# Packed attention and a three-way maximum layer on one core: the first two batches written in another order with other engines, and the steady batches written as one list for all engines

## The chip, the cores and the metric

The kernel runs on one core of a Trainium2 chip. The metric is the device time of one execution in microseconds (us). Before the change three runs took 495.62, 495.81 and 496.78 us.

In this text PE is the matrix engine (TensorE), DVE the vector engine, ACT the scalar engine, POOL GpSimd, and SP the engine that issues the DMAs. PSUM is the memory that PE writes its results to, SBUF the other on-chip memory.

## The reference

`q`, `k` and `v` have 8 batches, 8 heads, 576 positions and 64 columns; `p` has 32 packed queries per head. The packed queries attend to the 576 keys; every position's query then attends to the 32 packed results, which serve as keys and as values. The result, 4608 rows of 512, goes through a layer that takes the largest of three products and multiplies it by an output matrix:

```python
p_packed = sm_attn(p, k, v)
out = sm_attn(q, p_packed, p_packed)
x = out.transpose(0, 2, 1, 3).reshape(B * S, H * D)
h = np.maximum(np.maximum(x @ w1, x @ w2), x @ w3)   # 512 -> 768
return h @ w_out                                     # 768 -> 512
```

`sm_attn` is softmax attention with scale 1/8. All data is float32.

## The kernel before

**The work of one batch.** It is cut into stages, each a Python generator that issues a step at every `next`. A letter names the stage in the written order; the first digit behind it is the batch.

- S (`scores`): the packed queries against the keys, 32 narrow matmuls into two PSUM tiles, one for each parity r of the heads.
- A (`weigh`, and for batches 0 and 1 `turn`): maximum on DVE, exponential with its sum on ACT; in batches 0 and 1 a transposition on PE and copies out of PSUM. Z (`invert`): 1/sum on DVE.
- X (`spread`, batches 2 and on): two transpositions on DVE and 16 small DMAs that bring the weights into the layout of the value product.
- V (`values`): 80 narrow matmuls with v, scaled on DVE. K (`packed`): one transposition on PE and a copy. Q (`queries`): the packed results against q, 32 narrow matmuls.
- B (`attend`), for each r, eleven steps: transpositions (DVE), maximum (DVE), subtraction, exponential (ACT), sum (DVE), adding 1e-9, reciprocal (DVE), multiplication by it, transposition (DVE), rounding to a high part, and the low part as a difference. High and low part together carry float32 through fast matmuls.
- P (`project`), for each of six blocks j of the 768 hidden columns: the packed results times the three weights of that block, 16 narrow matmuls, then a high part on ACT and a low part on DVE. So the weights meet 32 packed rows instead of 576.
- N (`layer_in`), for each j six steps of six wide matmuls (two halves of the positions, three weights). E (`maximum`): a copy out of PSUM and two maxima on DVE, for each half.
- H (`halves`): sums and differences of pairs of blocks and their high and low parts, named ya, yb and yc. O (`layer_out`): 14 steps of nine wide matmuls on these (seven products in place of eight for each block of 2 by 2, in two columns m). F (`finish`): scaling and sums of the 14 results, and four stores.

Beside the batches, C (`convert`) makes float32 out of the weights' 64-bit words in four steps (ACT, ACT, DVE, POOL), and W (`weights`) prepares the output matrix's seven operands. k, v, q and w in the order are loads, issued by SP. I sets how many dummy matmuls on the identity PE does ahead of the next group.

**What sets the order.** The first two batches, with the start of the third and all weights, are a written list of words, `START`; the list is run under a manual schedule, so every engine's instructions stand in its order. A letter v, g or a behind a word puts that step on DVE, POOL or ACT in place of its default. Batches 2 to 7 go through a loop with a clock: each tick is one step of N or O, and `STAGES` says at which tick a stage of the next batch comes due (S at 7, X at 12, V at 29, Q at 36). There only PE's order is manual; the scheduler orders the other engines by its own estimate, and every step runs on its default engine: copies and casts on ACT (`copy`, L120 and L122), low parts on POOL (`split_lo`, L125), the subtraction of the maximum on POOL (L387), the multiplication by 1/z on DVE (L401), the differences in H on POOL (L505).

**Buffers.** PSUM has two pools: `ps_big`, two buffers of two banks, and `ps_moe`, four buffers of one bank, in which the results of N and O turn. A result's buffer comes free with the last instruction on DVE or ACT that reads it. Loads, hidden blocks and the spread weights share eight SBUF buffers (tag b), so a load can have to wait until an earlier product is through.

Of the kernel before, what the change touches and what calls it, by code (L numbers as in the profile page):

```python
# [22 lines left out]
P = 128  # L23
G = 2
# [24 lines left out]
k00 k01 I10 S0 A01 w02 w00 v00 C02 C02 A01 q010 A00 v01 A00 I7 A01 q000 A00 A01v A00v C02 q001 V01 C00 C00 V00  # L49
Z01 V01 Z00 V00 K0 K0v I1 Q0 w01 B000 C02 B010 C00 C01 C01 C01 q011 B010 B010 B010 B000 B000v B000 k10 C01 I8  # L50
Q0 B011 k11 B001 B001 B000 B000v w12 B010 C12 B000 B000 w11 I4 S1 v10 C00 I3 P00 B000 B000g v11 B001 w10 A10
A10 B001 B011 B011 B011 B010v q10 q11 A11 B010 P00 B001 B001 P00 P00 w21 A11 P00 k20 B010g B010 C12 C12 B000
I10 N00 C12 k21 A10 w20 Z10 B011 A10 w22 B010v B010 B011v B011 A11 A11 V101 B011g B001 C10 B001 w30 N00 C11
Z11 V101 C10 C10 C10 B011 C11 C11 C11 B001 B001v K1 B001 K1 Q1 B10 B011 B11 E000v C21 w32 B011v N00 E000 P01
P01 B11 C21 N00 N00 N00 P01 C21 S2 C21 E000 E001v E001 C20 C20 C20 C20 A20 C22 C22 N01 w42 N01 C22 E010 A20
w31 A21 E001 A21 C30 E010 C22 N01 N01 E010 w40 B10 C30 w41 P02 P02 C30 E011v P10 N01 P02 E011 C32 C32 N01 N02
C30 N02 C32 C32 C31 C31 C31 E011 X2 P10 C40 C40 N02 N02 w51 C31 B11v P10 E020v B10 C41 C41 C41 w50 P03 w62 C42
C42 C42 E020 v21 P03 C40 P11 P03 C50 E021 N02 N02 C41 v20 w52 E021 N03 E020 C40 N03 C51 E021 C42 B10 P04 E030v
C51 C51 w64 B10 w63 B11 B11 B11v X2 H00 C51 E030 N03 B10 B10 B11 P04 P04 H00g N03 E031 E030 N03 N03 E031 H01g
B11g X2 E031 N04 C64 B10 B10 B10g B10 H00 C52 N04 N04 B11 E040 N04 E040 E040 C50 B11v B11v C50 N04 P11 P11 C50  # L60
C63 C52 E041 C64 N04 N10 N10 E100 E100 w60 E041 C62 C63 C62 E041 H04 C52 H02 N10 N10 C52 w65 Z20 Z21 E101 N10
H02 C63 N10 N11 V201 C60 q20 P05 P05 C63 C62 E101 N11 V201 K2 K2 E101 C64 C64 E110v E110 P05 E100 q21 C62 H04v
W1v W1 H02v W1 N11 N11 E111 C65 C65 C65 N11 N11 E110 w61 Q2 B21 H03g C65 W1 W1 N05 N05 C60 B20 E050 N05 E050
H03v W2v W2v C61 C61 P12 C61 P12 P13 E111 C60 P13 N05 E051 N05 N05 P12 E051 E051 N12 C61 B20 C60 E111 N12 E050
P14 E120v N12 E120 P13 E120 W1 W1 H01v W0 W2 W2 H04 W0 B20v H01 P14 W0v W0g W0 H03v P14 N12 N12 N12 W1 N13 W2v
W2 W0v P20 H01 P15 E130 E121v E121 E121 N13 N13 E130 W0 N13 E131 E130 W1g W2v W2v H03 P15 P15 N13 k30 N13 E131
E131 N14 B20 N14 N14 E140 O0 H03g N14 H05v F0 E140 B20 B20v N14 N14 E141 N15 E141 E141 E140 O0 F0 O0 B21 B21
O0 B21 H13g H05 H05 H03v H05 N15 H01v E150 H01v B21 E150 N15 N15 E150 E151 W1v W0 H14 B20 H05g W2 H10v H10v
B21v B21 F0 N15 E151 P20 N15 E151 H14g H15 O0 O0 H05v O0 H13v W0g H11 F0 F0 O0 F0 W0v H12 O0 W2 F0 H11 F0 B21
O0 O0 F0 F0 O0 F0 F0 F0 F0 O0 O0 H12 H14 H10v H11v H11 H12v B20 H13 O1 H15v H15v H15v H13 H13v F1 O1 O1 H13  # L70
H15v F0 H11 F0 H11v H15v F1 F1 O1 O1 F1 B21 O1 F1 F1 O1 F1 O1 O1 F1 F1 k31 B21 B21v P20 B20 B20v O1 O1 B20v O1
O1 F1 F1 F1 F1 F1 O1 F1 F1
# [3 lines left out]
STAGES = "S1:7 P3:7 v1:9 X1:12 P4:18 P5:18 q1:26 V1:29 k2:31 K1:33 Q1:36 P6:40 P7:40 P8:45"  # L76
# [3 lines left out]
def fused_kernel(ctx: ExitStack, tc: tile.TileContext, kp, qt, va, vb, wi, wo, out):  # L80
# [529 lines left out]
    with tc.manual_schedule():  # L610
        for word in START.split():
# [5 lines left out]
            elif kind in loads:  # L617
                loads[kind](*x)
            else:
                if name not in begun:  # L620
                    begun[name] = stages[kind](*x)
                next(begun[name], None)
    chosen[0] = None


    clock, due = [0], []

    def begin(stage, at):
        due.append([at, len(due), stage])

    def tick():

        while True:
            ready = [d for d in due if d[2] is not None and d[0] <= clock[0]]
            if not ready:
                break
            d = min(ready, key=lambda d: d[:2])
            wait = next(d[2], None)
            while wait == 0:
                wait = next(d[2], None)  # L640
            if wait is None:
                d[2] = None
            else:
                d[0] = clock[0] + wait
        clock[0] += 1

    def both(f, b):
        def steps():
            for g in range(G):
                f(b, g)  # L650
            yield 0
# [92 lines left out]
```

## Time and profile before

| | before |
|---|---|
| median of three runs | 495.81 us (495.62 to 496.78) |
| the profiled execution | 495.07 us |
| its span, first to last instruction | 493.3 us |
| mean granted PE clock | 0.988 |
| PE busy | 469.0 us, 95% of the span |
| PE weight loads busy | 407.4 us, 83% |
| DVE busy | 319.3 us, 65% |
| ACT busy | 192.2 us, 39% |
| POOL busy | 286.1 us, 58% |

The span is 1.77 us shorter than the time of the execution that it was taken from. A view by line or tile gives for each group of instructions its tiles (out<-in, without buffer numbers), its shape, its count, its busy time, the mean of one, and after the bar the idle time of the engine ahead of it with what ended most of that. The view of waits says which engine and line waited for which, the total, the count and the longest. The chain of work starts at the last instruction and goes back at each step to what released it, or to the instruction ahead of it on its engine. The table of stretches gives each engine's busy time in a part of the span, with the number of instructions.

### The profile page before, as it was taken

Reading aid. Unit: us, or ns where it says so; the run is one execution under the profiler, and the core shown is the slowest. Engines: PE = TensorE matmul, PEld = TensorE weight load, DVE = VectorE, ACT = ScalarE, POOL = GpSimd, SP = SyncE. Lnnn points to the kernel's source line nnn. Section 1 sums busy time; section 2 is a strip of 40 time slices with the busy share of each in tenths; the row PEclk is TensorE's granted clock in tenths of the full one; section 3 lists DMA queues with packets and bytes.
Section 4 is the critical chain, followed back from the end, with each engine's and each line's share of the span. In section 5 each row is a group of like instructions: output and inputs, shape, how many; then the busy total and the mean of one; then the engine's idle time right before and its main releaser. Section 6 shows DMA issues by size and latency. Waiting matters only on the chain.

```text
span 493.3 us, 11594 instructions
## 1 busy us (share of the span) xinstructions
PE 469.0 (95%) x4710; PEld 407.4 (83%) x4710; DVE 319.3 (65%) x625; ACT 192.2 (39%) x374; POOL 286.1 (58%) x229
## 2 busy tenths in 40 slices
PE   8879988979887999999999999999999999999997
PEld 3347786768877989899998989899998999899996
DVE  2798997897987664586457565576457564673522
ACT  4266854322310153424434253524434353423430
POOL 0464868694971257652755566652756566644672
PEclk9998999899998999999999999999999999999999
DMA  8996846010013426015440426015430423011002
GB/s 314 385 398 246 269 133 228 3 52 2 25 48 94 163 44 190 35 37 157 99 155 25 145 55 209 17 49 151 114 133 25 152 53 110 3 58 41 1 0 97
DMA packets 36581, 55.67 MB, mean 113 GB/s; under 512 B 17328, under 2 KB 27568, under 8 KB 36528
## 3 DMA queue, kind: packets, MB, share of 16 engines
q1 hardware_dynamic: 36528, 54.93, 34.1%
q8 instruction: 37, 0.61, 0.5%
q14 instruction: 16, 0.13, 0.1%
HBM read 41.94 MB, written 9.44 MB: 104 GB/s over the span
## 4 chain that ended last, share of the span: by engine, by line
PE 76%; DVE 12%; DMA 5%; POOL 2%; ACT 2%; issue 2%; SPq 1%; DVEq 0%; ACTq 0%; POOLq 0%
PE mi L467 41%; PE mo L536 23%; PE pw L431 6%; DMA v<-in_va 2%; PE av L329 2%; PE s L358 2%; DMA q<-in_qt 1%; PE s L243 1%; DMA wi<-in_wo 1%; DVE r L481 1%; DVE r L505 1%; DVE ybl L125 1%; DVE ycl L125 1%; DVE pl L444 1%; ACT wi L178 1%
## 5 line engine op out<-in xcount | busy, mean ns | idle before, releaser
L467 PE MATMUL mi<-a2h,ph 128*128 128x288 f32 x576 | 175.8, 305 | 4.8 <-DVE r L122 2.0
L467 PE MATMUL mi<-a2h,pl 128*128 128x288 f32 x576 | 171.2, 297 | 0.8 <-DVE pl L444 0.6
L467 PE MATMUL mi<-a2l,ph 128*128 128x288 f32 x576 | 171.1, 297 | 0.0
L481 DVE TENSOR_TENSOR r<-mi,r 128x288 f32<-128x288 f32 x192 | 86.3, 453 | 79.5 <-PE mi L467 72.6
L467 PEld LDWEIGHTS mi<-a2h,ph 128*128 128x128 f32 x576 | 109.3, 190 | 22.6 <-issue 10.9
L505 POOL TENSOR_TENSOR r<-r 128x288 f32<-128x288 f32 (+1 forms) x67 | 71.3, 1065 | 78.1 <-DVE r L481 75.7
L467 PEld LDWEIGHTS mi<-a2h,pl 128*128 128x128 f32 x576 | 109.3, 190 | 1.3 <-DVE pl L444 1.2
L467 PEld LDWEIGHTS mi<-a2l,ph 128*128 128x128 f32 x576 | 109.2, 190 | 0.5 <-POOL a2l L125 0.2
L120 ACT COPY r<-mi 128x288 f32<-128x288 f32 x88 | 35.1, 399 | 117.5 <-PE mi L467 117.4
L444 DVE SCALAR_TENSOR_TENSOR pl<-pw,ph 128x768 fp32r<-128x768 f32 (+1 forms) x55 | 46.0, 847 | 22.8 <-ACT ph L442 22.8
L442 ACT ACTIVATE ph<-pw 128x768 fp32r<-128x768 f32 (+1 forms) x55 | 38.4, 726 | 19.0 <-PE pw L431 19.0
L125 POOL TENSOR_TENSOR ycl<-r,ych 128x864 fp32r<-128x864 f32 x19 | 39.2, 2065 | 8.5 <-ACT ych L120 6.1
L536 PE MATMUL mo<-ych,xh 128*128 128x288 f32 x144 | 43.6, 303 | 0.0
L431 PE MATMUL pw<-w_sb,pt 64*32 64x384 f32 x768 | 40.2, 490 | 2.7 <-DVE e L381 2.0
L536 PE MATMUL mo<-ych,xl 128*128 128x288 f32 x144 | 42.6, 296 | 0.0
L536 PE MATMUL mo<-ycl,xh 128*128 128x288 f32 x144 | 42.4, 295 | 0.1
L196 POOL TENSOR_TENSOR w_sb<-w_sb,wi 128x512 int32<-128x512 int32 x18 | 24.6, 1371 | 24.1 <-DVE z L272 11.6
L125 POOL TENSOR_TENSOR ybl<-r,ybh 128x576 fp32r<-128x576 f32 x20 | 29.5, 1476 | 11.8 <-ACT ybh L120 11.6
L125 POOL TENSOR_TENSOR yal<-r,yah 128x576 fp32r<-128x576 f32 x21 | 30.2, 1439 | 8.6 <-ACT yah L120 8.6
L125 POOL TENSOR_TENSOR a2l<-et,a2h 128x576 fp32r<-128x576 f32 (+1 forms) x14 | 18.2, 1300 | 26.0 <-ACT a2h L120 25.4
L536 PE MATMUL mo<-yah,xh 128*128 128x288 f32 x96 | 29.2, 304 | 3.8 <-DVE u L555 3.8
L536 PEld LDWEIGHTS mo<-ych,xh 128*128 128x128 f32 x144 | 27.0, 188 | 4.3 <-DVE u L555 3.1
(129 smaller groups left out, 821.4 us busy)
## 6 DMA issues: line engine op xcount, KB each, us to landing
kt<-in_kp SPq DMA_DIRECT2D x16, 640.0 KB, 5.8
wi<-in_wi SPq DMA_DIRECT2D x18, 512.0 KB, 7.1
v<-in_va SPq DMA_DIRECT2D x16, 512.0 KB, 5.5
q<-in_qt SPq DMA_DIRECT2D x14, 576.0 KB, 4.9
wi<-in_wo SPq DMA_DIRECT2D x6, 512.0 KB, 5.9
out_t<-r SPq DMA_DIRECT2D x8, 288.0 KB, 2.2
out_t<-t SPq DMA_DIRECT2D x8, 288.0 KB, 2.3
out_t<-s SPq DMA_DIRECT2D x8, 288.0 KB, 2.3
```

The costliest lines, as they stand in the source:

```text
L120: e.copy(out=out, in_=src)
L125: on(default).tensor_tensor(out=lo, in0=src, in1=hi.bitcast(F32), op=ALU.subtract)
L196: nc.gpsimd.tensor_tensor(out=dst.bitcast(I32), in0=dst.bitcast(I32), in1=up, op=ALU.add)
L329: nc.tensor.matmul(out=ps[r][NP * i:NP * i + NP, :], lhsT=at[r][0:n, t, i], rhs=loaded["v", b, g][0:n, t, h * D:(h + 1) * D], start=(t == ...
L358: nc.tensor.matmul(out=s2[b][hf][32 * n:32 * n + 32, r, 0:HS], lhsT=pt_sb[b % 2][o, NP * n:NP * n + NP], rhs=q[g][o, pr, hf * HS:(hf + 1) ...
L431: nc.tensor.matmul(out=ps[r][NP * n:NP * n + NP, 0:NW * P], lhsT=pt_sb[b % 2][o, NP * n:NP * n + NP], rhs=w_sb[o, j, n * NW * P:(n + 1) * ...
L442: nc.scalar.activation(out=hi[:, r], in_=x, func=AF.Copy, scale=2.0 ** -WS)
L444: nc.vector.scalar_tensor_tensor(out=lo[:, r], in0=x, scalar=2.0 ** -WS, in1=hi[:, r].bitcast(F32), op0=ALU.mult, op1=ALU.subtract,)
L467: nc.tensor.matmul(out=sums[b, j, hf, x][:, 0:HS], lhsT=w[:, r, x * P:(x + 1) * P], rhs=a[:, c], start=(r == 0 and n == 0), stop=(r == R - ...
L481: nc.vector.tensor_tensor(out=h, in0=sums[b, j, hf, i][:, 0:HS], in1=h, op=ALU.max)
L505: less = lambda out, x, y: on("g").tensor_tensor(out=out, in0=x, in1=y, op=ALU.subtract)
L536: nc.tensor.matmul(out=ps[:, 0:HS], lhsT=w[:, x, m * P:(m + 1) * P], rhs=h[:, z], start=(p == 0 and i == 0), stop=(p == NQ - 1 and i == 2),)
```

## The change

`START` is written anew: the same steps of the same batches in another order, with other engines for part of the copies, casts, low parts, sums and differences. It also holds two projections of batch 2 (P21, P22) that the loop issued before. `STAGES`, the clock, and the functions that serve it are gone. In their place stands a second list, `LOOP`, which holds one batch of N, E, H, O and F with the loads, scores, values, queries, attention and projections that belong to the next one (digit 1 for the next batch, 0 for this one). `run` goes through a list word by word with the batch added, and all engines keep its order. In `project`, block 0 of every batch but batch 1 now takes two buffers of `ps_moe` in place of one of `ps_big`, with a high and a low part for each r. No computation is added or removed.

```diff
 START = """
-k00 k01 I10 S0 A01 w02 w00 v00 C02 C02 A01 q010 A00 v01 A00 I7 A01 q000 A00 A01v A00v C02 q001 V01 C00 C00 V00
-Z01 V01 Z00 V00 K0 K0v I1 Q0 w01 B000 C02 B010 C00 C01 C01 C01 q011 B010 B010 B010 B000 B000v B000 k10 C01 I8
...
+k00 k01 w02 I10 S0 A00 A00 k10 w00 C00 k11 Z00 w22 A00 w01 A01 A01 v01 Z01 C00 C02 C00 C01 v00 I4 S1 A10 A10
+q000 C00 A11 I7 A01 A01v V01 C02 C02 A00v Z10 C01 C01 V01 q010 V00 C02 V00 K0 A11 Z11 C01 C22 C22 C22 K0 I1 Q0
...
-STAGES = "S1:7 P3:7 v1:9 X1:12 P4:18 P5:18 q1:26 V1:29 k2:31 K1:33 Q1:36 P6:40 P7:40 P8:45"
+LOOP = """
+S1 A10 N00 N01 E000 A10 A11 Z10 N00 E010v A11 N01 N01 X1 X1 N01 E000 E010 N02 N01 E011 N00 E011 E000 N00 N00
+E001v E001 v11 N00 N02 E001 H00 E020v Z11 v10 X1 N02 N02 E020 E020 q11 N02 E021 N02 E021 N01 E011 E021 P04
...
+"""
@@ project
-        if j == 0 and b == 0 or j == 3 and b >= 2:
+        if j == 0 and b != 1 or j == 3 and b >= 2:
@@ fused_kernel
-    with tc.manual_schedule():
-        for word in START.split():
+    def run(words, base):
+        for word in words.split():
             name = word.rstrip("vga")
             chosen[0] = word[len(name):] or None
             kind, x = name[0], [int(i) for i in name[1:]]
             if kind == "I":
                 idle[0] = int(name[1:])
-            elif kind in loads:
+                continue
+            if kind not in "wCW":
+                x[0] += base
+                if x[0] >= B:
+                    continue
+            if kind in loads:
                 loads[kind](*x)
             else:
...
-    clock, due = [0], []
-    def begin(stage, at):
-    def tick():
-    def both(f, b):
-    def issue(name, b, at):
-    with tc.manual_schedule(engines={mybir.EngineType.PE}):
-        for b in range(2, B):
...
+    with tc.manual_schedule():
+        run(START, 0)
         for b in range(2, B):
+            run(LOOP, b)
```

**The first loads on SP.** kt0 and kt1 are batch 0's keys, kt2 and kt3 those of batch 1; v0, v1, q0 and q1 belong to batch 0; wi0_2 is part 2 of weight block 0. Before:

```order
L149 DMA kt0_79<-in_kp 128x1280
L149 DMA kt1_81<-in_kp 128x1280
L143 DMA wi0_2_108<-in_wi 128x512
L143 DMA wi0_0_110<-in_wi 128x512
L155 DMA v0_112<-in_va 128x1024
L156 DMA v0_112<-in_vb 64x256
L164 DMA q1_120<-in_qt 128x2x288
L155 DMA v1_126<-in_va 128x1024
L156 DMA v1_126<-in_vb 64x256
```

The same queue after the change:

```order
L158 DMA kt0_79<-in_kp 128x1280
L158 DMA kt1_81<-in_kp 128x1280
L152 DMA wi0_2_83<-in_wi 128x512
L158 DMA kt2_113<-in_kp 128x1280
L152 DMA wi0_0_115<-in_wi 128x512
L158 DMA kt3_118<-in_kp 128x1280
L152 DMA wi2_2_123<-in_wi 128x512
L152 DMA wi0_1_132<-in_wi 128x512
L164 DMA v1_141<-in_va 128x1024
L165 DMA v1_141<-in_vb 64x256
L164 DMA v0_151<-in_va 128x1024
L165 DMA v0_151<-in_vb 64x256
```

Two key tiles of batch 1 and two more weight blocks now stand ahead of both value tiles of batch 0.

**PE in a steady batch,** around the projections of blocks 4 and 5 of batch 3 (pw3_4, pw3_5); mi are the layer-in results. Before:

```order
L467 MATMUL mi3_2_1_2_3008<-a2h3_1_2700,pl3_2_2728 128x288
L467 MATMUL mi3_2_1_2_3008<-a2l3_1_2702,ph3_2_2727 128x288
L431 MATMUL pw3_4_3016<-w_sb_72,pt1_74 32x384 x8
L431 MATMUL pw3_5_3025<-w_sb_72,pt1_74 32x384 x8
L467 MATMUL mi3_3_0_0_3036<-a2h3_0_2682,ph3_3_2879 128x288
L467 MATMUL mi3_3_0_0_3036<-a2h3_0_2682,pl3_3_2880 128x288
```

After the change, with av4 the values of batch 4, whose 80 matmuls and the eight of block 3 are cut here to their first and last rows:

```order
L476 MATMUL mi3_1_1_2_2984<-a2l3_1_2756,ph3_1_2563 128x288
L440 MATMUL pw3_4_2993<-w_sb_72,pt1_74 32x384 x8
L440 MATMUL pw3_3_0_3010<-w_sb_72,pt1_74 32x384
L440 MATMUL pw3_3_1_3011<-w_sb_72,pt1_74 32x384
...
L338 MATMUL av4_3024<-v8_2930,xt4_2933 32x64 x2
L338 MATMUL av4_3024<-v9_2906,xt4_2933 32x64 x2
...
L440 MATMUL pw3_5_3070<-w_sb_72,pt1_74 32x384 x8
L476 MATMUL mi3_4_0_0_3079<-a2h3_0_2669,ph3_4_3005 128x288
```

Block 3's projection and the values of the next batch now stand between blocks 4 and 5 in one run of narrow matmuls; before, block 3 followed the scores and the values stood alone among layer-in products. The last two projections of the next batch's opening three stood among O's products and now all three stand ahead of them.

**DVE in a steady batch,** from the end of layer in on (r3 are hidden blocks of batch 3, e4, z2_4 and pl4 attention and projection parts of batch 4). Before:

```order
L481 TENSOR_TENSOR r3_2_3104<-mi3_5_1_2_3255,r3_2_3104 128x288
L381 STREAM_TRANSPOSE e4_0_3306<-s2_4_0_3263 128x288
L381 STREAM_TRANSPOSE e4_0_3306<-s2_4_1_3272 128x288
L385 TENSOR_REDUCE m2_4_0_0_3323<-e4_0_3306 128x18
L381 STREAM_TRANSPOSE e4_1_3326<-s2_4_0_3263 128x288
L381 STREAM_TRANSPOSE e4_1_3326<-s2_4_1_3272 128x288
L385 TENSOR_REDUCE m2_4_1_0_3341<-e4_1_3326 128x18
L392 TENSOR_REDUCE z2_4_0_0_3396<-e4_0_3306 128x18
L444 SCALAR_TENSOR_TENSOR pl4_0_3377<-pw4_0_3344,ph4_0_3376 128x768
```

After the change, from the last maximum of layer in to the low part of yc of the second pair of blocks:

```order
L490 TENSOR_TENSOR r3_1_2925<-mi3_3_1_2_3280,r3_1_2925 128x288
L396 TENSOR_TENSOR e4_1_3151<-e4_1_3151,m2_4_1_0_3248 128x576
L134 TENSOR_TENSOR yal3_1_3290<-r3_1_2925,yah3_1_3250 128x576
L408 RECIPROCAL z2_4_0_0_3219<-z2_4_0_0_3219 128x18
L514 TENSOR_TENSOR r3_2_3100<-r3_2_3100 128x2x288
L453 SCALAR_TENSOR_TENSOR pl4_0_3324<-pw4_0_0_3308,ph4_0_3323 128x384
L453 SCALAR_TENSOR_TENSOR pl4_0_3324<-pw4_0_1_3309,ph4_0_3323 128x384
L514 TENSOR_TENSOR r3_1_2925<-r3_1_2925 128x2x288
L410 TENSOR_TENSOR e4_0_3156<-e4_0_3156,z2_4_0_0_3219 128x576
L131 CAST ych3_2_3378<-r3_2_3100 128x864
L134 TENSOR_TENSOR ycl3_1_3384<-r3_1_2925,ych3_1_3382 128x864
```

DVE's subtraction, two low parts, two differences and a cast of hidden blocks stood on POOL and ACT before; they now stand in DVE's queue between the last maximum of block 3 and the low part that the output products read.

More of the change, by code (lines that the diff above doesn't have):

```diff
@@ L631, in tick @@
-    def tick():
[L633 to L645, printed above, removed]
-    def both(f, b):
[L648 to L651, printed above, removed]
-        return steps()
@@ L679, in fused_kernel @@
[L679 to L700 removed]
+                key = (kind, *x)
@@ L704 @@
+                if key not in begun:
+                    begun[key] = stages[kind](*x)
+                next(begun[key], None)
+        chosen[0] = None
+    with tc.manual_schedule():
+        run(START, 0)
+        for b in range(2, B):
+            run(LOOP, b)
 def kernel(q, k, v, p, moe_w1, moe_w2, moe_w3, moe_w_out):
```

97 lines of the change are left out of this document (28 added, 69 removed).

## The prediction

> **What bounds the kernel now.** I read the page's head first, then the table of busy time by stretch, the waits of PE, the chain of work that ended last, and single tiles. The head gives the span and PE's share:
>
> ```profile
> span 493.3 us, 11594 instructions
> PE 469.0 (95%) x4710; PEld 407.4 (83%) x4710; DVE 319.3 (65%) x625; ACT 192.2 (39%) x374; POOL 286.1 (58%) x229
> ```
>
> PE is the bound, and it is idle for 24.3 us in all. Where, the stretch table says (length, then busy time of PE, weight loads, DVE, ACT and POOL, then granted clock, DMA share, GB/s). The first row is the written opening up to the first layer-in product of batch 2, the second is batches 2 to 6, the third batch 7:
>
> ```profile
> 0.00:166.54 166.54, 145.78 (x1407) 114.68 (x1408) 135.88 (x250) 68.39 (x130) 100.43 (x89) 0.97 0.48 167
> 166.54:441.35 274.81, 274.77 (x2917) 246.79 (x2917) 164.56 (x337) 108.78 (x215) 157.81 (x121) 1.00 0.31 94
> 441.35:493.30 51.95, 48.43 (x390) 45.89 (x389) 18.85 (x40) 15.00 (x29) 27.84 (x21) 0.99 0.12 41
> ```
>
> Steady batches (54.96 us each) have no PE idle time to win, 0.04 us in five; the opening has 20.76 us of it. The opening in finer steps, same columns:
>
> ```profile
> 0.00:26.60 26.60, 22.93 (x230) 9.82 (x230) 14.34 (x41) 10.16 (x22) 7.68 (x14) 1.00 0.96 349
> 26.60:42.05 15.45, 12.67 (x175) 9.65 (x175) 14.27 (x34) 10.24 (x21) 8.53 (x9) 0.89 0.93 370
> 42.05:76.18 34.13, 32.11 (x299) 26.99 (x298) 31.81 (x62) 23.49 (x44) 24.37 (x21) 1.00 0.66 205
> 76.18:86.93 10.75, 8.59 (x161) 6.10 (x160) 8.11 (x16) 4.98 (x8) 9.21 (x9) 0.96 0.63 216
> 86.93:114.21 27.28, 23.90 (x215) 19.27 (x215) 24.78 (x39) 8.71 (x15) 22.10 (x17) 0.95 0.08 25
> 114.21:140.00 25.79, 24.00 (x180) 22.75 (x179) 20.47 (x33) 6.86 (x14) 17.82 (x15) 1.00 0.04 13
> 140.00:166.54 26.54, 21.59 (x156) 20.10 (x155) 22.10 (x29) 3.94 (x7) 10.72 (x8) 0.94 0.28 92
> ```
>
> DVE is 92% busy from 26.6 to 114.2 (14.27 + 31.81 + 8.11 + 24.78 of 87.6 us), ACT about half: the opening is bound by DVE, with PE waiting on its results. PE's longest waits agree: DVE names three of these four, a load of q the other.
>
> ```profile
> PE mo L536 <- DVE u L555: 3.8, 1, 3.8
> PE s L358 <- DMA q<-in_qt: 2.2, 1, 2.2
> PE mi L467 <- DVE r L122: 2.0, 1, 2.0
> PE pw L431 <- DVE e L381: 2.0, 1, 2.0
> ```
>
> **The change, part by part.**
>
> *The first loads.* How long the loads take, and when their users start (KB each and us to landing; then stretches with GB/s last; then two PE rows):
>
> ```profile
> kt<-in_kp SPq DMA_DIRECT2D x16, 640.0 KB, 5.8
> wi<-in_wi SPq DMA_DIRECT2D x18, 512.0 KB, 7.1
> v<-in_va SPq DMA_DIRECT2D x16, 512.0 KB, 5.5
> ```
> ```profile
> 0.00:13.13 13.13, 10.24 (x56) 4.52 (x56) 3.97 (x11) 5.45 (x10) 0.92 (x7) 1.00 0.88 311
> 13.13:20.00 6.87, 6.27 (x117) 2.98 (x117) 4.23 (x13) 1.78 (x4) 2.33 (x3) 1.00 1.05 402
> ```
> ```profile
> 13.13 1.72 PE L329 MATMUL pa<-v,a1t 128*32 128x64 f32 x76 [1.12 <-DMA v<-in_va]
> 26.60 0.37 PE L467 MATMUL mi<-a2h,ph 128*128 128x288 f32 x1 [0.18 <-ACT z L395]
> ```
>
> Batch 0's value product needs both v tiles. SP now issues them behind four k tiles and four weight blocks: 4 x 640 + 4 x 512 + 2 x (512 + 64) KB = 5760 KB, 5.9 MB. By 13.13 us 311 GB/s have moved 4.1 MB; the rest at 402 GB/s takes 4.5 us. So batch 0's values start near 17.6 instead of 13.1, and its first layer-in product near 31.1 instead of 26.6. Against that the scores of batch 2 (1.13 us) now lie ahead of that product, so PE is behind by 3.4 us. I take +3.4; bounds +4.5 (no credit) and 0 (everything behind is DVE's queue, which the early scores of batch 1 feed sooner).
>
> *Engines of the opening's steps.* By count of words, DVE loses five multiplications by 1/z (now on POOL), two subtractions of the maximum, four z additions, five casts of layer results and two casts and two splits of batches 0 to 2, and gains eight splits or differences of layer results and weights and four copies out of PSUM. At 0.4 to 1.2 us each by their size (the rows below give 0.46 and 0.77 for a multiplication of 288 and 576 columns) that is some -14 and +9.5: about -4 us of DVE work. POOL loses about 8 us, ACT takes 11 more, with room (68.39 of 166.54). Less POOL work also means fewer collisions:
>
> ```profile
> L401 DVE TENSOR_TENSOR e<-e,z x15: 457/774/2300, 22.7 to 435.2; 128x576 f32<-128x576 f32 x13, 128x288 f32<-128x288 f32 x2
> L125 POOL TENSOR_TENSOR ycl<-r,ych 128x864 fp32r<-128x864 f32 x19 | 39.2, 2065 | 8.5 <-ACT ych L120 6.1 <-DVE ych L122 1.8
> ```
> ```profile
> 143.51 1.98 DVE L401 TENSOR_TENSOR e<-e,z 128x576 f32<-128x576 f32 x1
> ```
>
> The same DVE multiplication takes 0.77 at the median and up to 2.30 us; 2.30 is about one POOL split of 2.07 us more. The Trainium skill, "SBUF — State Buffer", section "Who interferes with whom", explains it: a DVE instruction with two SBUF inputs and a POOL instruction that reads SBUF exclude each other for the whole instruction; the rows agree. Where DVE is saturated, its saved work is saved time: I take -4, with bounds 0 (the chain is latency, not work) and -7 (3 us of collisions go too).
>
> *The wait for q of batch 2.* The load starts only when batch 2's values release their buffer, and PE has little to do in between; behind the wait the clock is low:
>
> ```profile
> 78.23 7.08 DMA q<-in_qt
> 85.31 0.04 issue
> 85.35 1.58 PE s L358 x24
> 86.93 2.93 PE mi L467 x12
> ```
>
> Cost: 2.2 us of wait, 24 score matmuls in 1.58 instead of 24/32 x 1.13 = 0.85, and 12 wide ones in 2.93 instead of 12 x 0.133 = 1.6: 4.3 us. In the new list PE has eleven layer-in steps (11 x 6 x 0.133 = 8.8 us) and DVE some 11 us between those values and these queries, against four steps, a projection and 5 us of PE work that the list of before has at that place; 7.08 us of load is then covered. I take -4.2; bounds -4.3 and 0 (SP's queue holds the load back behind weight blocks that wait for POOL).
>
> *The end of the opening* (140 to 166.54): 4.95 us idle and a clock of 0.94, another 1.6 us: 6.5 us. These are the waits for DVE's splits and sums. The new list gives 16 of the opening's 18 casts of layer results to ACT (5 before), but piles all of batch 1's last layer, three projections and batch 2's attention between the fourth and fifth output products. I take a third, -2.2, with bounds -6.5 and +2 (the pile's own wait, the size of today's second-longest).
>
> *Steady batches.* Pieces of the chain in one batch (start, length):
>
> ```profile
> 227.06 1.13 PE s L243 x32
> 228.19 0.65 PE pw L431 x16
> 228.84 9.01 PE mi L467 x66
> 237.85 1.45 PE pw L431 x32
> ...
> 253.10 2.40 PE mi L467 x18
> 255.50 1.13 PE s L358 x32
> ...
> 269.47 0.81 PE pw L431 x16
> ```
>
> A projection costs 0.81 alone but 0.65 behind other narrow matmuls, and wide ones run at 2.40/18 = 0.133 undisturbed but 9.01 for 66 (8.80 + 0.21) behind a narrow group. Each narrow group dropped saves 0.16 + 0.21 = 0.37 us. The scheduler's order had six groups per batch; the written list has four (scores; two projections, values, projection; queries; three projections). That is -0.74 in five batches and -0.37 in the last: -4.1. It also brings the values nearer to the transposed weights they need:
>
> ```profile
> 233.14 10.39 SPq L309 DMA_DIRECT2D xt<-x  x16
> ```
> ```profile
> DMA to landing us min/median/max: 1.9/2.0/4.1
> ```
>
> SP takes 0.65 us for each of 16 copies. In the list DVE's second transposition ends some 5.6 us after the scores begin (two maxima 1.4, exponentials on ACT, two copies, two transpositions at 0.77); plus 10.39 and 2.0, minus one copy's issue, is 17.4. PE wants them after 1.13 + 18 x 0.8 + 0.81 + 0.65 plus re-entries, 17.1. A wait of 0.3 us in each of five batches: +1.5, bounds 0 and 1.2 each. The Trainium skill, "DMA: Bandwidth & Descriptors", section "Issuing engines are not separate DMA queues", calls the sequencer's time to start a DMA usually small beside the DMA; by that the 1.5 would be 0. The trace disagrees: 10.39 us of issue against 2.0 of landing.
>
> DVE's work per batch rises by about 9 us, from 32.9 to 42 of 54.2: copies, splits and differences from ACT and POOL at 0.45 to 1.05. It hides under PE while each result stays ahead of its matmul (rival 1).
>
> Sum: +3.4 - 4 - 4.2 - 2.2 - 4.1 + 1.5 = -9.6. The profiled execution took 495.07 us with a span of 493.3; 485.5 for it. The median of three runs, 495.81, lies 0.74 above it: **486.2**.
>
> **The rivals.**
>
> *1. The steady list is too tight (slower).* DVE's two-SBUF-input instructions rise from 2 to 10 per batch while POOL stays at work for about 25 of 54 us. The place: from layer 3's last product to the seventh output product PE has three projections and six products, 2.1 + 6 x 1.2 = 9.3 us. DVE must in that time do a maximum, a subtraction, two differences, two splits, two projection splits, a multiplication and a cast, about 7.3 us at clear prices. One collision with the 2.07 us split eats the 2 us of slack, a second stops PE. Every us of stall costs 6 us in the kernel; the change loses above 1.6 us per batch beyond the 0.3. At 2.2 us: 486.2 + 13 = 499. For it: the 2300 ns maximum; against: POOL's own work falls from 31 to about 25 us per batch. The section on who interferes speaks for this rival.
>
> *2. The early delay is never made up.* If chain latency rather than DVE work sets the opening, the +4.5 stays, the q wait hides in it, and DVE's relief is worth nothing: 495.81 + 4.5 - 2.6 = 497.7. For it: ACT and PE wait in turn until 42 us; against: DVE at 92%.
>
> *3. The opening closes up.* All bounds on the good side: 0 - 7 - 4.3 - 6.5 - 4.1 = -22, with half of them reached 478. For it: DVE's clear work is well under 166 us; against: DVE stays the most loaded engine there.
>
> **How the numbers follow.** A measurement of this kernel can tell about 0.3%, 1.5 us, from no change. Forecast 0.63 (480 to 492 by its bounds), rival 3 0.10, rival 2 0.12, rival 1 0.15. Faster: 0.63 + 0.10 and a little of rival 1 with milder stalls, 0.75. Same: a part of rival 2, 0.07. Slower: 0.18. The range reaches down to rival 3 and up to rival 2: 478 to 497.5.
>
> **What would show it.** In the changed profile: the first layer-in product near 31 us; no wait for q at batch 2's queries; the first layer-in of batch 2 near 159 to 162 us, two projections earlier in the order than today; steady batches at 54.2 to 54.6 us with one wait of about 0.3 for the transposed weights; DVE near 42 us per batch. Wrong would be PE waits for ycl or for PSUM copies in every batch, DVE rows of 2 us there, a batch over 55 us, or an opening that is still DVE-bound and longer than 166 us.

## The result, and the profile after

The changed kernel takes 481.33 us (median of four runs, 478.06 to 483.5) against 495.72 us of the kernel before (four runs, 494.97 to 496.78): a ratio of 0.9703, 95% interval 0.9644 to 0.9761. That is 14.4 us faster where 9.6 were forecast. The profiled execution, the slowest of the four, took 483.5 us with a span of 481.3. Its page begins like this:

```profile
span 481.3 us, 11535 instructions
PE 463.0 (96%) x4710; PEld 406.7 (84%) x4710; DVE 341.2 (71%) x707; ACT 160.9 (33%) x325; POOL 236.4 (49%) x208
```

The span is 12.0 us shorter and PE's busy time 6.0 with the same 4710 matmuls, so half of it was idle time of PE and half matmuls that ran closer together. To see where, I cut the span at the end of the opening, at batch 7 and at its end. The opening's end is the first matmul after the last output product of batch 1 at which batch 2's three projections are also done: 166.54 before, 150.21 now. The columns are those of the table of stretches in the prediction.

```profile
0.00:150.21 150.21, 139.85 (x1413) 112.91 (x1421) 114.70 (x242) 76.62 (x144) 88.59 (x85) 0.97 0.51 181
150.21:427.70 277.49, 274.74 (x2917) 247.65 (x2918) 200.29 (x417) 74.33 (x160) 126.16 (x106) 1.00 0.31 95
427.70:481.30 53.60, 48.43 (x391) 46.17 (x389) 26.19 (x49) 9.99 (x21) 21.64 (x18) 0.99 0.11 38
```

Against the three rows of before: opening 166.54 to 150.21, **-16.3**; batches 2 to 6 274.81 to 277.49, **+2.7**; batch 7 51.95 to 53.60, **+1.7**. The whole gain lies in the opening; the written list for the steady batches gave 4.3 us back, where the prediction had it win 2.6. In the opening PE's idle time falls from 20.76 to 10.36 us and its busy time from 145.78 to 139.85. The mean granted clock is 0.97 in both openings, so it does not explain the 5.9 us of busy time; what does was not found. Now the opening in finer steps:

```profile
0.00:31.83 31.83, 24.97 (x261) 11.41 (x262) 14.60 (x43) 13.46 (x29) 10.35 (x17) 0.89 0.97 353
31.83:69.40 37.57, 35.87 (x418) 28.70 (x416) 34.48 (x77) 29.16 (x56) 28.48 (x27) 1.00 0.73 254
69.40:83.82 14.42, 12.74 (x148) 11.93 (x147) 9.02 (x24) 5.76 (x11) 8.44 (x8) 0.88 0.67 245
83.82:103.27 19.45, 19.33 (x205) 16.01 (x205) 17.90 (x31) 11.09 (x18) 13.85 (x13) 1.00 0.01 2
103.27:150.21 46.94, 46.94 (x388) 44.85 (x394) 38.70 (x70) 17.16 (x31) 27.48 (x24) 1.00 0.18 60
```

The first layer-in product comes at 31.83 us (26.60 before). From 83.82, where batch 2's queries start, PE is idle for 0.12 us in 66.39 (19.45 - 19.33, then 0.00). Before, those queries started at 85.35, and the three stretches from 86.93 to 166.54 held 10.12 us of idle time and clocks of 0.95, 1.00 and 0.94. So nearly all of the 16.3 us is won behind batch 2's queries. No wait for q is left. The waits of PE in the five steady batches are two groups, neither of which was there before:

```profile
PE mo L545 <- ACT s L561: 1.7, 5, 0.4
PE av L338 <- DMA xt<-x: 0.9, 3, 0.4
```

One steady batch in the chain of work that ended last, from its scores to the next batch's (start, length, what):

```profile
261.41 1.13 PE s L252 x32
262.54 14.65 PE mi L476 x108
277.19 1.45 PE pw L440 x32
278.94 1.51 PE av L338 x69
280.54 0.64 PE pw L440 x12
281.18 4.25 PE mi L476 x30
...
297.21 1.56 PE pw L440 x32
299.05 0.66 ACT ybh L129
299.71 2.17 ACT ph L451 x4
302.23 14.60 PE mo L545 x108
316.83 1.13 PE s L252 x32
```

It takes 55.42 us (316.83 - 261.41), where the prediction's pieces of before had 54.95 (282.01, where the next scores start, less 227.06):

```profile
282.01 1.13 PE s L243 x32
```

The two stops are seen in the rows of after: the values go on only at 278.94 after projections that end at 278.64, and ACT's four high parts (`ph`) stand in the chain between the last projection and the output products. (Before, the three projections stood among the output products, two behind the fourth and one behind the ninth; now all three stand ahead of the first.) SP's row of the same batch:

```profile
266.81 10.67 SPq L318 DMA_DIRECT2D xt<-x  x16
```

### The profile page after: what moved, and what is told of

It is laid out like the page before. It is cut to its first block, busy times and chain, and to the rows that moved or that the text cites. A ratio compares the mean times of both kernels' runs of the same rounds, so it can differ in the third digit from the quotient of the medians.

```text
span 481.3 us, 11535 instructions
## 1 busy us (share of the span) xinstructions
PE 463.0 (96%) x4710; PEld 406.7 (84%) x4710; DVE 341.2 (71%) x707; ACT 160.9 (33%) x325; POOL 236.4 (49%) x208
## 4 chain that ended last, share of the span: by engine, by line
PE 72%; DMA 9%; SPq 6%; DVE 4%; ACT 4%; issue 2%; POOL 1%; DVEq 0%; ACTq 0%; POOLq 0%
PE mi L476 36%; PE mo L545 26%; SPq L318 6%; PE pw L440 5%; DMA wi<-in_wi 4%; ACT ph L451 2%; DMA v<-in_va 2%; PE s L367 2%; PE av L338 2%; DMA wi<-in_wo 2%; DMA xt<-x 1%; PE s L252 1%; DVE r L490 1%; PE s L142 1%; ACT ybh L129 1%
## 5 line engine op out<-in xcount | busy, mean ns | idle before, releaser
L490 DVE TENSOR_TENSOR r<-mi,r 128x288 f32<-128x288 f32 x192 | 83.3, 450 | 52.7 <-PE mi L476 42.4
L514 POOL TENSOR_TENSOR r<-r 128x288 f32<-128x288 f32 (+1 forms) x47 | 49.2, 1055 | 77.6 <-DVE r L490 74.0
L129 ACT COPY r<-mi 128x288 f32<-128x288 f32 x66 | 25.6, 397 | 177.3 <-PE mi L476 174.2
L545 PE MATMUL mo<-ych,xh 128*128 128x288 f32 x144 | 42.6, 296 | 0.0
L440 PE MATMUL pw<-w_sb,pt 64*32 64x384 f32 x768 | 37.5, 488 | 0.4 <-POOL w_sb L205 0.4
L134 POOL TENSOR_TENSOR yal<-r,yah 128x576 fp32r<-128x576 f32 x14 | 20.0, 1427 | 30.6 <-ACT yah L129 30.1
L134 POOL TENSOR_TENSOR ycl<-r,ych 128x864 fp32r<-128x864 f32 x12 | 28.2, 2347 | 12.1 <-DVE ych L131 12.1
L545 PE MATMUL mo<-yal,xh 128*128 128x288 f32 x96 | 28.4, 295 | 0.6 <-DVE yal L134 0.6
L545 PE MATMUL mo<-yah,xl 128*128 128x288 f32 x96 | 28.3, 295 | 0.0
L545 PE MATMUL mo<-ybl,xh 128*128 128x288 f32 x96 | 28.3, 295 | 0.0
```

The costliest lines, as they stand in the source:

```text
L129: e.copy(out=out, in_=src)
L134: on(default).tensor_tensor(out=lo, in0=src, in1=hi.bitcast(F32), op=ALU.subtract)
L440: nc.tensor.matmul(out=ps[r][NP * n:NP * n + NP, 0:NW * P], lhsT=pt_sb[b % 2][o, NP * n:NP * n + NP], rhs=w_sb[o, j, n * NW * P:(n + 1) * ...
L490: nc.vector.tensor_tensor(out=h, in0=sums[b, j, hf, i][:, 0:HS], in1=h, op=ALU.max)
L514: less = lambda out, x, y: on("g").tensor_tensor(out=out, in0=x, in1=y, op=ALU.subtract)
L545: nc.tensor.matmul(out=ps[:, 0:HS], lhsT=w[:, x, m * P:(m + 1) * P], rhs=h[:, z], start=(p == 0 and i == 0), stop=(p == NQ - 1 and i == 2),)
```

## The experiments

The theory from these traces: the new opening gives all of the gain, the written list takes 4 us back, by two waits that can be mended. The rivals: the list gives a part of the gain; the longer batches come from how the opening ends; the opening's gain is that of its engines alone, or of its order alone. Each ratio below is to the kernel before, run on the same chip in the same session; medians of before were 494.6 in the first session, 496.47 in the second, 495.72 in the third.

| run | us (median) | ratio, 95% interval |
|---|---|---|
| new opening, old loop | 478.32 | 0.9656, 0.9599 to 0.9713 |
| old opening, new list | 501.75 | 1.0135, 1.0095 to 1.0174 |
| new order, old engines in the opening | 503.71 | 1.0183, 1.0139 to 1.0228 |
| old order, new engines in the opening | 504.06 | 1.0187, 1.0146 to 1.0227 |
| the changed kernel again | 481.70 | 0.9700, 0.9672 to 0.9728 |
| spread weights earlier | 479.26 | 0.9656, 0.9627 to 0.9685 |
| spread weights and scaling earlier | 476.15 | 0.9598, 0.9569 to 0.9626 |
| before, without the wait for q | 497.53 | 1.0027, 1.0004 to 1.0049 |
| attention's 20 letters old | 487.73 | 0.9835, 0.9782 to 0.9888 |
| halves' 27 letters old | 494.40 | 0.9977, 0.9951 to 1.0003 |
| maxima's and weights' 28 letters old | 488.62 | 0.9868, 0.9822 to 0.9913 |
| batch 0's values loaded first | 482.09 | 0.9728, 0.9694 to 0.9762 |

**The two halves of the change.** First the new opening in front of the old loop:

```diff
-LOOP = """
...
+STAGES = "S1:7 P3:7 v1:9 X1:12 P4:18 P5:18 q1:26 V1:29 k2:31 K1:33 Q1:36 P6:40 P7:40 P8:45"
...
-        if j == 0 and b != 1 or j == 3 and b >= 2:
+        if j == 0 and b in (0, 2) or j == 3 and b >= 2:
...
-            run(LOOP, b)
+            for x in STAGES.split():
+                name, at = x.split(":")
+                issue(name, b, clock[0] + int(at))
...
```

> The new opening with the old steady loop (STAGES, the scheduler orders the other engines). Theory (the traces: the opening with equal content ends 16.3 us earlier, all that follows takes 4.3 us longer): the whole gain is the opening's and the written list costs about 4, so this kernel is faster than the changed one by about 4 us: 477, steady batches of 54.9 to 55.0 us and a last one of 52. Rival A (the longer batches are owed to how the opening ends, not to the list): 481, as the changed kernel, batches of 55.5. Rival B (my forecast's terms: the list saves 2.6 and the opening the rest): 484.

Measured: 478.32. Rows of its chain of work (the first layer-in of batch 2 behind its first two matmuls, which started at 150.64, and a stop of 0.73 us for attention's low part; then two scores of steady batches):

```profile
151.79 5.57 PE mi L467 x40
...
212.31 1.13 PE s L243 x32
...
267.27 1.13 PE s L243 x32
```

The steady batch is 54.96 us again, and from 151.79, where PE goes on, to the span's end of 478.3 are 326.5 us, about the 326.8 of before (493.3 - 166.54). By the trace the old loop behind the new opening is better than the list by the expected 4 us; by the times its interval overlaps with that of the changed kernel, so they alone would not tell. Rivals A and B fall by the length of the batches. Then the list behind the old opening, whose last words are followed by the two projections that the list expects:

```diff
 O1 F1 F1 F1 F1 F1 O1 F1 F1
+P21 P21 P22 P21 P22 P22
...
-        if j == 0 and b != 1 or j == 3 and b >= 2:
+        if j == 0 and b not in (1, 2) or j == 3 and b >= 2:
```

> The old opening, with the two projections P21 and P22 appended to it, and the new written list for batches 2 to 7. Theory: the list alone costs about 4 us: 500, steady batches near 55.5 us and a last one near 53.6. Rival A (the longer batches come from the new opening's end): 495 to 496. Rival B (the list alone saves 2.6, as forecast): 493.

Measured: 501.75, 7 us slower than before. Its chain, first scores in the list and two steady batches:

```profile
166.27 1.20 PE s L251 x30
...
221.75 1.13 PE s L251 x32
...
277.64 1.13 PE s L251 x32
```

The opening ends where it did (166.27, with two stops of 1.5 us in all at the seam, for the low parts of the two appended projections), batches take 55.5 and 55.9 us, and the rest is 331.8 us (498.1 - 166.27), 5.0 longer than before. The list costs its time behind either opening.

**Engines or order.** The new and the old opening give 75 steps to different engines. First all of them back, in the new order (a piece of it):

```diff
-H15 B21 H11v H11v H13v H13 F0 H13v P20 H11 H11 P20 P20 H15
+H15v B21v H11 H11v H13 H13v F0 H13 P20 H11 H11 P20 P20 H15v
```

and the same 75 letters, the other way round, put into the old order:

```diff
-H12 H14 H10v H11v H11 H12v B20 H13 O1 H15v H15v H15v H13 H13v
+H12 H14v H10v H11v H11 H12v B20g H13v O1 H15v H15 H15 H13v H13
```

> The changed kernel, but each step of the opening on the engine that the old opening gave it (75 letters changed back); the order is the new one. Theory C (the order makes the opening short: PE is given work ahead of what it waits for): at most a third of the 16 us comes back, 482 to 486. Theory D (the engines do it: DVE's relief and fewer collisions of DVE with POOL, whose busy times fell by 21 and 12 us): 490 to 496.

> The kernel before, but each step of the opening on the engine that the new opening gives it (75 letters changed); order and steady loop are the old ones. Theory C (order): 492 to 496, within 3 us of the kernel before. Theory D (engines): 481 to 488.

Measured: 503.71 and 504.06. Both theories fall, and in a way neither had thought of: each half alone makes the kernel 9 us slower than before, where both together make it 14 faster. (The first of the two also has the new list: what follows its opening takes 333.4 us, 6.6 longer than before, so most of its 9 us is the list's. The second has the old loop. The other PSUM buffers for block 0 of batch 2 went with the order and were not tried alone.) The stretch up to the end of the opening, first new order with old engines, then old order with new engines:

```profile
0.00:167.93 167.93, 144.51 (x1406) 115.66 (x1406) 123.31 (x245) 68.90 (x131) 97.97 (x89) 0.95 0.46 162
```
```profile
0.00:175.90 175.90, 147.99 (x1406) 116.67 (x1407) 124.66 (x242) 75.89 (x143) 89.53 (x85) 0.92 0.44 155
```

In both DVE is busy for 11 to 13 us less than the 135.88 of before, and both openings are longer than its 166.54, by 1.4 and 9.4. What sets the opening's length is thus not how long DVE is busy.

Nor is DVE's busy time its work alone. The same instructions take longer in one opening than in another; the conversion of the output weights' words before, then after:

```profile
L192 DVE TENSOR_SCALAR xb<-wi 128x512 uint32<-128x512 uint32 x6 | 5.5, 922 | 0.5 <-DMA xt<-x 0.5
```
```profile
L201 DVE TENSOR_SCALAR xb<-wi 128x512 uint32<-128x512 uint32 x6 | 2.5, 428 | 2.3 <-ACT wi L187 2.3
```

I count the DVE instructions that take over 0.3 us longer than the shortest with the same tiles and shapes in any trace, and sum what they take beyond it: before, 32 instructions in the opening with 26.2 us, and each of them runs for more than half of its time beside a POOL instruction; after, 8 with 6.2 us. So 20 of the 21.2 us by which DVE's busy time fell is time that its instructions lost beside POOL's (I call it collisions), and hardly any of it is work. The new order with the old engines has 15.9 us of this, the old order with the new engines 16.4: 10 less than before in both, and neither opening is shorter.

That left the question whether one group of steps carries it. The theory now: every engine takes its steps in order, and letters and order fit only together, so that each group changed back costs its part (M); the rival: the gain is that of the multiplications by 1/z, which collide with POOL's work (L). Three kernels change one group of letters back, each in the new order; a piece of each, the 20 letters of B and K first, then the 27 of H, then the 28 of E and W:

```diff
-C22 C22 C22 K0 I1 Q0 B000 C22 B000 B000
+C22 C22 C22 K0v I1 Q0 B000 C22 B000 B000v
...
-H11v H11v H13v H13 F0 H13v P20
+H11 H11v H13 H13v F0 H13 P20
...
-W2g N12 E121 E121 W0v H01 W1 W1 W1 H02 N13 E121 N13 E130v
+W2 N12 E121v E121 W0 H01 W1 W1 W1 H02 N13 E121 N13 E130
```

> The changed kernel with the 20 letters of the attention steps (B) and the packed copies (K) of its opening changed back to the old engines; order and all other letters new. All 75 letters changed back cost 22 us (503.71). Theory M (each engine takes its steps in order, so letters and order fit only together, and every group of letters costs its part): 485 to 490. Theory L (the multiplications by 1/z back on DVE bring its collisions with POOL back, and those were the gain): 495 or more here, and under 484 for the other two groups.

> The changed kernel with the 27 letters of the casts, splits and differences of layer results (H) in its opening changed back. Theory M: 486 to 492. Theory L: under 484.

> The changed kernel with the 28 letters of the maxima's first copies (E) and of the output weights (W) in its opening changed back. Theory M: 485 to 490. Theory L: under 484.

Measured: 487.73, 494.40 and 488.62. By the ratios they lie 1.4, 2.8 and 1.7% of the time before above the changed kernel's 0.9700, some 7, 14 and 8 us; the sum, 29, is somewhat more than the 24 of all together (1.0183 - 0.9700). L falls: attention's letters are the cheapest group, and the halves' the dearest, at 494.4 a little beyond M's 486 to 492. The opening with the old letters of H, and with those of E and W:

```profile
0.00:163.64 163.64, 143.85 (x1413) 115.88 (x1420) 119.27 (x242) 69.23 (x133) 100.19 (x96) 0.95 0.48 166
```
```profile
0.00:156.34 156.34, 141.60 (x1413) 113.73 (x1419) 114.45 (x236) 77.50 (x147) 94.51 (x88) 0.96 0.49 174
```

With the old letters of E and W, DVE is busy for 114.45 us, as in the changed kernel (114.70), and the opening is 6.1 us longer all the same. So DVE's busy time does not set this opening's length either.

A wider form of L stays untested, that the collisions of all steps carry the gain. In the new order they are the more, the longer the opening is: 6.2 us in the 150.2 of the changed kernel, 6.1 in 152.3 with attention's letters old, 11.0 in 156.3 with those of E and W, 11.7 in 163.6 with those of H, and 15.9 in 167.9 with all of them. The old order does not fit in: it has 26.2 us in 166.5 and, with the new engines, 16.4 in 175.9. No run changes the collisions alone.

**The wait for q.** Would the kernel before have won its 4.2 us without that wait?

```diff
-Q2 B21 H03g C65 W1 W1 N05 N05 C60 B20 E050 N05 E050 H03v
+H03g C65 W1 W1 N05 N05 C60 E050 N05 Q2 B21 B20 E050 H03v
```

> The kernel before, with the queries of batch 2 (and the first transposition of its result on DVE) moved behind one more layer-in step of layer 5 than before (three instead of two, about 0.8 us, and POOL's and ACT's words in between), all else as it was. My step 'each stop of PE in the opening is paid in full': the wait for q shrinks by 1 to 2 us, 493 (-1.5). Rival (the opening is one chain through all engines, fitted by hand: what is later on it costs, whatever PE does meanwhile): no gain or a loss, 495 to 497.

The edit is larger than this text says: the queries move behind three layer-in steps, none of which stood ahead of them before; that is 2.4 us of PE work and covers the whole wait. Measured: 497.53, a ratio of 1.0027: slower, if by little. The waits of PE from 76 to 168 us in the kernel before, then in this one:

```profile
PE s L358 <- DMA q<-in_qt: 2.2, 1, 2.2
...
PE mi L467 <- DVE r L481: 1.2, 2, 0.6
```
```profile
PE mi L466 <- DVE r L480: 2.5, 4, 0.9
...
PE pw L430 <- DVE e L380: 1.1, 1, 1.1
PE mi L466 <- ACT r L119: 1.1, 1, 1.1
```

The wait for q is gone, and its 2.2 us come back as waits for DVE's maxima (1.2 to 2.5), for attention's transposition (1.1) and for ACT's copy (1.1). As I read it, queries that come later delay the rest of attention, and the layer-in products that fill the hole use up PSUM buffers earlier; no run sets these apart. The rival was right. The Trainium skill, "Perfetto Trace Analysis", section "Optimization Strategies", advises to work on the engines that block the critical path while PE waits; here one such wait was taken away and the time did not fall, since waits of the same size came up elsewhere.

**The first loads.** Batch 0's values ahead of batch 1's keys again, with the rest of the new opening kept:

```diff
-k00 k01 w02 I10 S0 A00 A00 k10 w00 C00 k11 Z00 w22 A00 w01 A01 A01 v01 Z01 C00 C02 C00 C01 v00 I4
+k00 k01 w02 I10 S0 A00 A00 w00 C00 v01 v00 Z00 k10 A00 k11 A01 A01 w22 Z01 C00 w01 C02 C00 C01 I4
```

> The changed kernel with batch 0's two v tiles loaded ahead of batch 1's k tiles and of two weight blocks, as in the kernel before. My step 'the early loads cost 3.4 us': the first layer-in product near 27 to 28 us, and 478 (-3.4). Rival (the early scores of batch 1 feed DVE and ACT while they are idle and pay for the later values): the first layer-in is earlier, but the opening's end is not, 481 to 484.

Measured: 482.09, as the changed kernel. PE no longer waits for v but for the keys, and the first layer-in product starts at the same place (the view of waits, then a row of PE's timeline):

```profile
PE s L251 <- DMA kt<-in_kp: 2.2, 2, 1.8
```
```profile
31.88 0.48 PE L475 MATMUL mi<-a2h,ph 128*128 128x288 f32 x1
```

Neither side had it: the first layer-in product is not earlier at all. In the new list batch 1's scores stand ahead of batch 0's values on PE, so PE needs the keys first, whichever is loaded first. The DMA engines are 97% busy up to 31.83 us in the changed kernel; that the sum of loads ahead of that product sets its time, and not their order, fits both runs, but no run with fewer loads was made.

**The two waits of the list.** The changed kernel once more, then with the two transpositions X ahead of DVE's copy and reciprocal, so that SP's copies start earlier, then also with the first scaling F0 ahead of ACT's high part of projection P12 (the second pair of lines):

```diff
-S1 A10 N00 N01 E000 A10 A11 Z10 N00 E010v A11 N01 N01 X1 X1 N01 E000
+S1 A10 N00 N01 E000 A10 A11 N00 A11 X1 X1 Z10 E010 N01 N01 N01 E000
...
-H03 P12 P12 O0 F0 O0 P10
+H03 P12 O0 F0 P12 O0 P10
```

> The changed kernel itself, once more, beside the two edits of its list and on their chip. 481 to 482, opening of 150 us, steady batches of 55.4 to 55.8 us with a stop of 1.3 us at the values (0.36 of it put down to the spread weights) and one of 0.35 at the output products. If the old loop behind the new opening (478.32 against 494.6) is really better than the written list, the ratio here is above 0.9656 by 0.004 to 0.008.

> The changed kernel with the two transpositions X of batch b+1 ahead of DVE's copy and reciprocal in the written list (that copy goes to ACT), so that SP's 16 copies begin about 0.5 us earlier. Theory (the value product waits at the end of SP's 16 issues): the stop at the values goes, batches of 55.0 us instead of 55.42, 479.0 (-2.3). Rival (the stop is the price of a value product among projections, as in every list): batches stay at 55.4, 481.3.

> The same, and the first scaling of an output product ahead of the high part of the third projection in ACT's queue. Theory (the third-last stop of PE is for a PSUM buffer that waits for ACT, behind four high parts): both stops go, batches of 54.5 to 54.6, as forecast for the list, and 477 (-4.3). Rival: the fourth output product waits for another buffer then (the projection's), 479, as with the first edit alone.

Measured: 481.70, 479.26 and 476.15, close to the three numbers of the theory (the changed kernel's ratio of 0.9700 lies 0.0044 above that of the old loop, as expected); the last one's interval lies clear of the changed kernel's, the middle one's touches it. Scores and values of one steady batch and the next scores, from the chain of the kernel with the first edit, and SP's row:

```profile
256.81 1.13 PE s L252 x32
...
274.03 1.47 PE av L338 x80
...
311.91 1.13 PE s L252 x32
```
```profile
261.66 10.78 SPq L318 DMA_DIRECT2D xt<-x  x16
```

SP begins 4.85 us after the scores (261.66 - 256.81), where the changed kernel had 5.40 (266.81 - 261.41); the 80 matmuls of the values run in one piece behind the projections, and the batch takes 55.10 us, 0.32 less than 55.42 (over four batches of each trace, 0.3 to 0.4 less). With both edits:

```profile
257.67 1.13 PE s L252 x32
...
293.20 2.10 PE pw L440 x48
295.30 16.89 PE mo L545 x126
312.19 1.13 PE s L252 x32
```

Now the output products follow the projections at once, and the batch takes 54.52 us, another 0.58 less and 0.43 less than the 54.95 of before. The stop that went, in the changed kernel's PE row, with the last product ahead of it:

```profile
301.59 0.29 PE L545 MATMUL mo<-yal,xh 128*128 128x288 f32 x1
302.23 0.41 PE L545 MATMUL mo<-yah,xh 128*128 128x288 f32 x1 [0.35 <-ACT s L561]
302.47 0.30 PE L545 MATMUL mo<-yah,xl 128*128 128x288 f32 x1
```

It is the third output product that waits, not the fourth, as the expectation has it: 18 of 126 matmuls run ahead of the stop. Undisturbed, these starts lie 0.133 us apart; here 0.88 us pass in place of 0.27. So the stop costs 0.61 us, of which 0.35 are named as a wait, and this is about the 0.58 that its removal gave.

This kernel, the new opening with the mended list, has the lowest median of all: 0.9598 of the time before, against 0.9656 of the new opening with the old loop, with overlapping intervals. The traces do not show the mended list to be better than the old loop: from the opening's end (148.26) to the span's end (474.9) it takes 326.6 us, where the old loop takes 326.8 and, behind the new opening, 326.5. Its five steady batches are 1.8 us shorter (273.0 against 274.8), and its last batch is 1.7 longer (53.6 against 51.95).

## Why the prediction was right, and where it was not

The direction and the size were near (486.2 forecast, 481.33 measured, 478 to 497.5 the range). The sum came near by luck, with two errors against each other. By the trace:

| | forecast | measured in the span |
|---|---|---|
| opening: +3.4 - 4 - 4.2 - 2.2 | -7.0 | -16.3 |
| five steady batches: 5 x (-0.74 + 0.3) | -2.2 | +2.7 |
| batch 7 | -0.4 | +1.7 |
| sum | -9.6 | -12.0 |

The medians differ by 2.4 us more than the two spans, since the profiled execution of after was its slowest and that of before lay below its median.

*The first loads, +3.4.* The place held: first layer-in forecast at 31.1, found at 31.83. The reason did not: with the values first, the product starts at 31.88 all the same. So it was not v's place in SP's queue alone; that all loads ahead of the product set its time is argued, not shown.

*Engines of the opening's steps, -4.* This is the step that failed, and its premise with it. I read "the opening is bound by DVE" from 92% busy time (the four rows give 78.97 of 87.6 us, which is 90%) and made DVE's saved work saved time. DVE's busy time fell far more than I had summed, from 135.88 to 114.70, nearly all of it collisions, for which I had allowed 3 us at the bound. But the runs show that this busy time does not set the length: the old order with the new engines relieves DVE by 11 us and lengthens the opening by 9.4; the old letters of E and W leave DVE's busy time where it is and cost 6.1. The section "Who interferes with whom" of "SBUF — State Buffer" in the Trainium skill explains collisions, and the trace agrees with it: each of the 32 long instructions in the opening of before ran beside POOL's. No run here shows them to be the gain. (The 2.30 us of the multiplication, which I called a whole split more, is 1.5 us above its median: the split had begun 0.37 us earlier, at 319.23 against 319.60. It also lies in steady batches, where PE did not wait.)

*The wait for q, -4.2.* The wait went, as said. But the 4.2 is not a term of its own: taken out of the kernel before it gave nothing (1.0027). I had costed a stop of PE at its length without asking what is late next. (The list of before has five layer-in steps at that place, not four.)

*The end of the opening, -2.2.* The largest miss by size. I credited a third of 6.5 us, and only of the last 26 us. The new list takes out nearly all of it from 83.82 on: 10.12 us of idle time down to 0.12, and the clocks of 0.95 and 0.94 there up to 1.00. Rival 3 had this part right: all bounds on the good side gave the opening -17.8, and it came to -16.3. (Half of the way from the forecast to all bounds is 480, not the 478 stated there.) The chance of 0.10 for it was too small, for the prediction argued from DVE's load that the opening could not close up.

*Narrow groups, -0.74 per batch.* The term exists but is smaller: with both waits mended the batch is 0.43 shorter than before. The pieces of the chains show why. Wide matmuls took 46.84 us of a batch before (9.01, 8.93, 3.38, 2.40, 4.96, 6.42, 6.18 and 5.56) and take 46.34 in the kernel with both edits (14.66, 4.24, 0.80, 9.75 and 16.89): 0.25 for each of the two groups less, about the 0.21 that I had put on a re-entry. The narrow ones took 8.01 and take 8.07 (the projections among them 4.36 and 4.33), so the 0.16 that I had credited for each group dropped did not come.

*The wait for the spread weights, +0.3 per batch.* Right, in place, cause and size, though the trace names it in three of the five batches only: 0.4 us at the longest, 0.32 when it was taken away. The Trainium skill, "DMA: Bandwidth & Descriptors", section "Issuing engines are not separate DMA queues", has the time to initiate a DMA as usually small; by that nothing would have been gained, and SP's 10.67 us for 16 copies decide.

*What the sum lacked:* the wait of the third output product for a PSUM buffer, 0.58 us per batch, or 2.9 in five: with three projections run ahead of the output products, ACT has their four high parts in its queue ahead of the scaling that frees the buffer. Rival 1 named the place, and "PE waits for PSUM copies in every batch" stood there as a sign of being wrong, but it put the blame on DVE's collisions with POOL. DVE is busy for 40.1 us per batch (200.29 / 5) and is in neither of the two groups of waits. A batch over 55 us, the other sign of being wrong that the prediction named, was there.

*Batch 7, +1.7.* Up to the start of DVE's last instruction the rows below give 48.61 us before and 49.43 after with equal PE work (48.43), so 0.8 us is idle time of PE: two waits for DVE's results, 0.4 and 0.6 us, are in the trace. The other 0.8 us lie behind that instruction, where only stores are left: 2.9 us to the end of the span before (493.3 - 490.42), 3.7 after (481.3 - 477.59). Why the stores end later was not tried.

```profile
489.96 0.46 DVE u L555
```
```profile
477.13 0.46 DVE u L564
```

What stays open is why the new order and the new engines fit each other. The runs show that neither serves without the other and that every group of letters costs its part; no single queue or wait was found that carries it, and fewer collisions of DVE with POOL remain a rival in the new order.

## What to carry to other kernels

In a stretch where all engines take turns in fixed orders, an engine's busy share does not price its work, and a stop of PE does not price its removal: ask what is late next, and measure an order and its engine choices only together, never one with the other's. In a list that repeats, follow each stop to the queue of the engine that ends it: two moves of a few words, read from SP's and ACT's queues, brought a list that cost 4 us level with the loop that it replaced.

## What the runs showed of the hardware

The 16 copies that spread a batch's weights take SP 10.4 to 11.7 us in the kernel before and 10.4 to 11.4 in the changed one, against about 2 us from issue to landing: here a queue of small copies is an engine's work like any other. A stop can cost more than the wait that the trace names: the output products' wait of 0.35 us cost 0.61 by its rows, since the first two matmuls behind it start later than the wait alone makes them. A DVE instruction's time depends on what POOL does beside it: the six conversions of the output weights' words took 0.92 us each before and 0.43 after. And the same opening ended at 150.21, 148.65, 148.26 and 146.3 us in four profiled executions (the changed kernel twice, the one with both edits, and the one with the first edit; each the start of its first scores in the list, the last by PE's timeline):

```profile
148.65 1.13 PE s L252 x32
```
```profile
148.26 1.13 PE s L252 x32
```
```profile
146.30 1.20 PE L252 MATMUL s<-kt 64*32 64x288 f32 x32
```

So a difference of up to 4 us between two openings needs more than one trace, while the steady batches of the kernel before, where no wait stands in them, agree within 0.1 us (54.95 to 54.99).
